# Attention, a three-way-maximum layer and a gated layer on one core: the whole first layer moved behind the attention, quarter-array products for the last keys, wider exponentials

## The chip, the cores and the metric

The kernel runs on one core of a Trainium2 chip. The metric is the device time of one execution in microseconds; lower is better. Engines are named as in the profile: PE is TensorE (matrix products; PEld its weight loads), DVE is VectorE, ACT is ScalarE, POOL is GpSimd, SP the queue from which nearly all DMAs are issued. Every matrix product of the program streams 384 or 448 columns. An fp32 matmul shows as two weight loads and two MATMUL records; a product in fp32r shows as one of each.

## The reference

```python
scores = q @ k.T / 8;  scores = 30 * tanh(scores / 30)     # 4 batches x 12 heads, 448 x 448
attn = exp(scores - max);  attn /= attn.sum(-1) + 1e-9
x = (attn @ v).transpose(0, 2, 1, 3).reshape(1792, 768)
h = maximum(maximum(x @ w1, x @ w2), x @ w3)               # first layer, 768 -> 768
y = h @ w_out                                              # second layer, 768 -> 768
out = (sigmoid(y @ w_gate) * (y @ w_val)) @ w_out2         # third 768 -> 1536, fourth 1536 -> 768
```

The weights arrive as eight-byte floats, and are decoded on ACT and DVE (five instructions a block) to fp32. Every product of the layers is split in high and low fp32r halves, and takes three passes (high x high, high x low, low x high).

## The kernel before, in words

**Attention.** A batch has 448 rows: three groups of 128 keys and a rest of 64. Heads go in pairs, 24 in all, and a pair's two heads lie in partitions 0 to 63 and 64 to 127. `scores` (L296 on) gives, per pair, one full-array product for the rest of the keys (L312) and three groups of two half-array products (L315; each head uses its 64 rows of the array and its own PSUM bank). ACT takes tanh of each of the four results (L320), then exp (L334). `weigh` (L346 on) multiplies the weights with v, two column halves of the array at a time (L353); `total` (L356 on) sums the weights over the keys with a matrix of ones (L364; the first six pairs also L362 for the rest, later pairs add the rest on DVE, L343). `finish` (L367 on) transposes the totals on DVE, takes the reciprocal and multiplies. For the last eight pairs q and k are split, and the scores take three fp32r passes.

**First layer before.** `Layer1` does batches 0 and 1 as plain products: for each of 6 column blocks j and 3 matrices, 18 matmuls per batch (648 in all). They are interleaved with the attention from pair 7 on, and the last of them run just behind it. `Layer1Pair` then does batches 2 and 3 as seven block products (Strassen-Winograd): nine triples of column-block pair and matrix, each of 7 products of 9 matmuls (567 in all, L556). A block product needs sums of the two batches' halves (`making`, `cut`, L973 to L985) and sums of the weights' quarters (L527 to L530), each split in high and low (L535, L536).

**Order.** `PROGRAM` writes out, by letters and per pair, in which order PE, DVE and ACT get their instructions (`manual_schedule`): F is `finish`, S storing x split, U adding up the sums, 1 the first sum, P, W and O a plain first-layer product, its weights and its evacuation, d one third of a decoding, X the next pair's preparation. 24 weight blocks are decoded during the attention, and 8 more after it. DMAs wait in the SP queue in the order of issue. Everything after the attention is ordered by the scheduler's priorities.

**Block products.** `Blocks.run` (L540 on) goes through the triples; `prepare` splits the weights of a product into a ring of three buffers, two products ahead; `after` evacuates: ACT copies three of the seven results (L575), DVE adds three (L580), and `out` takes the maximum on DVE. `hooks` hang other work behind a named product.

Of the kernel before, what the change touches and what calls it, by code (L numbers as in the profile page):

```python
# [17 lines left out]
def tile_kernel(ctx: ExitStack, tc: tile.TileContext, q, k, v, cap, w1, w2, w3, wo, wg, wv, wo2, out):  # L18
# [15 lines left out]
    MAKING = (1, 1, 1, 1, 1, 1, 1, 1, 1, 1, 1, 1)  # L34
    ROOMS = {1: 8, 2: 9, 6: 10, 5: 11, 7: 12, 3: 13, 4: 14}
    SOON = 24
    ONESX = (0, 1, 2, 3, 4, 5)
# [3 lines left out]
        0: ("", "d1UddXd"),  # L41
        1: ("", "1FXUS"),
        2: ("dd", "F1SUXd"),
        3: ("d1d", "FUSXd"),
        4: ("dd", "d1FSUX"),
        5: ("dd1", "FSdUX"),
        6: ("dd", "1FSUXdd"),
        7: ("F1", "BdPSWUdOX"),
        8: ("ddF", "PS1WUdXO"),
        9: ("ddFd1", "PXWSUOd"),  # L50
        10: ("ddF", "1PXWSUdO"),
        11: ("ddF", "1WSPXUddO"),
        12: ("dF", "d1PXWSUddO"),
        13: ("ddF1", "PWSOPXWUddddO"),
        14: ("ddF", "W1PSOPXWUddddO"),
        15: ("ddF", "P1WSOPXWUdO"),
        16: ("dF", "Sd1PWOXPWUdO"),
        17: ("ddF", "1PWSOPXWUO"),
        18: ("ddF", "1PWXSUOPWddO"),
        19: ("dd", "F1PWSOPXWUdO"),  # L60
        20: ("dF1", "PWSOPXWUdO"),
        21: ("d", "F1PWSOPXWOU"),
        22: ("F", "1PWSOPXWUO"),
        23: ("Fd", "1PWSOPWUOPXWO"),
        24: ("d", "FPWSOPWOPWO"),
    }
    PLAIN = (0, 1, 2, 3, 4, 5, 6, 7, 8, 9, 10, 11, 12, 13, 14, 15)
# [5 lines left out]
    us = dram.tile([B, NF, P, S], F32, name="us")  # L73
    ws2 = dram.tile([NF, P, DM], F32, name="ws2")
# [87 lines left out]
    class Rooms:  # L162
# [5 lines left out]
        def flat(self, n, name, dt=F32R):  # L168
            return self.pools[n // 8].tile([P, KC * S], dt, tag=f"room{n}", name=name, bufs=1)
# [27 lines left out]
    def load_pair(n, pools, begin=None):  # L197
        ld, wk, ep, pp, mm, (ident, ones, onesx, capb, tsc, kfs, vss, vts) = pools
# [12 lines left out]
        nc.sync.dma_start(out=kf[:, : NT * P], in_=kk[:, : NT * P])  # L211
# [3 lines left out]
        for e in range(2):  # L215
            own = slice(e * D, (e + 1) * D)
            nc.sync.dma_start(out=kf[own, NT * P + e * TAIL : NT * P + (e + 1) * TAIL], in_=kk[own, NT * P :])
        nc.sync.dma_start(out=vs, in_=main(v))
        for e in range(2):
            nc.sync.dma_start(out=vx[e * TAIL : (e + 1) * TAIL, e], in_=rest(v)[e])  # L220
        return qf, kf

    def prepare(n, loaded, pools):


        ld, wk, ep, pp, mm, (ident, ones, onesx, capb, tsc, kfs, vss, vts) = pools
        qf, kf = loaded
        if n in PLAIN:
            return kf, qf
        kh = wk.tile([P, SK], F32R, tag="kh", name="kh")  # L230
        nc.scalar.copy(kh, kf)
        kl = wk.tile([P, SK], F32R, tag="kl", name="kl")
        nc.vector.tensor_sub(kl, kf, f(kh))
        qh = wk.tile([P, S], F32R, tag="qh", name="qh")
        nc.scalar.copy(qh, qf)
        ql = wk.tile([P, S], F32R, tag="ql", name="ql")
        nc.vector.tensor_sub(ql, qf, f(qh))
        return kh, kl, qh, ql

# [4 lines left out]
    def less_max(es, pools):  # L244

        ld, wk, ep, pp, mm, (ident, ones, onesx, capb, tsc, kfs, vss, vts) = pools
        for e in es:
            nc.vector.tensor_scalar_mul(e, e, capb)
        for h in range(2):
# [4 lines left out]
            top = pp.tile([P, 512], F32, tag="pv", name="top", bufs=2)  # L254
            for c in range(NT + 1):
                cols = slice(c * P, min((c + 1) * P, S))
                n = cols.stop - cols.start
                turned = pp.tile([P, 2, 512], F32, tag="sc", name="turned")[:, 0]
# [23 lines left out]
    class Pair:  # L282


        def __init__(self, n, prepared, pools, xb, general):
            self.n, self.prepared, self.pools, self.xb, self.general = n, prepared, pools, xb, general
            self.e, self.sum = {}, None

            self.alone = n < NP and not general
            self.whole = n in ONESX and not general  # L290
            self.own = general

        def scores(self, groups, add=True):

            ld, wk, ep, pp, mm, (ident, ones, onesx, capb, tsc, kfs, vss, vts) = self.pools
            if self.n in PLAIN:  # L296
                terms = (self.prepared,)
            else:
                kh, kl, qh, ql = self.prepared
                terms = ((kh, qh), (kl, qh), (kh, ql))  # L300
            last = len(terms) - 1
            banks = []
            for c in groups:
                if c is None and not self.own:
                    pool, tag = (mm, "mm") if self.n <= NP else (pp, "pv")
                    sc = pool.tile([P, 512], F32, tag=tag, name="rest", bufs=2).unsqueeze(1)
                else:
                    sc = pp.tile([P, 2, 512], F32, tag="sc", name="sc")
                banks.append(sc)
                for m, (kk, qq) in enumerate(terms):  # L310
                    if c is None:
                        nc.tensor.matmul(sc[:, 0, :S], kk[:, NT * P : SK], qq, start=(m == 0), stop=(m == last))  # L312
                        continue
                    for j, own in enumerate(HALVES):
                        nc.tensor.matmul(sc[:, j, :S], kk[own, c * P : (c + 1) * P], qq[own], start=(m == 0), stop=(m == last))  # L315
            for c, sc in zip(groups, banks):
                w = 1 if c is None else 2
                e = ep.tile([P, w, S], F32, tag=f"e{w}", name="e", bufs=7 if w == 2 else 3)
                self.e[c] = e
                nc.scalar.activation(e, sc[:, :w, :S], AF.Tanh, scale=tsc)  # L320
            if not self.general:
                for c in groups:
                    self.weights(c, add)

        def add_first(self):
            ld, wk, ep, pp, mm, (ident, ones, onesx, capb, tsc, kfs, vss, vts) = self.pools
            self.sum = ep.tile([P, 2, S], F32, tag="sum", name="sum", bufs=2)
            nc.vector.tensor_add(self.sum, self.e[0], self.e[1])

        def weights(self, c, add=True):  # L330

            ld, wk, ep, pp, mm, (ident, ones, onesx, capb, tsc, kfs, vss, vts) = self.pools
            e = self.e[c]
            nc.scalar.activation(e, e, AF.Exp, scale=1.0 if self.general else capb)  # L334
            if c == 1 and add:
                self.add_first()

        def add_up(self):
            nc.vector.tensor_add(self.sum, self.sum, self.e[2])
            if self.whole:  # L340
                return
            for j, own in enumerate(HALVES):
                nc.vector.tensor_add(self.sum[own, j], self.sum[own, j], self.e[None][own, 0])  # L343
# [11 lines left out]
        def total(self):  # L355

            ld, wk, ep, pp, mm, (ident, ones, onesx, capb, tsc, kfs, vss, vts) = self.pools
            if self.alone:
                self.pv.append(mm.tile([P, 512], F32, tag="mm", name="pv"))
# [6 lines left out]
        def finish(self):  # L366
# [6 lines left out]
            if self.general:  # L373
                nc.vector.tensor_scalar_add(inv, r[:, :, 0], 1e-9)
# [450 lines left out]
    def compute(own: ExitStack, general, once):  # L825
# [138 lines left out]
        for _ in ahead:  # L964
            pass
# [247 lines left out]
```

## Time and profile before

| | us |
|---|---|
| median of 3 runs | 1003.03 (1000.75 to 1008.34) |
| profiled execution, its own time | 1000.76 |
| its span | 998.9 |
| PE busy | 984.5 |
| DVE busy | 783.0 |
| ACT busy | 532.6 |
| POOL busy | 43.3 |
| first scores start | 5.23 |
| Layer1Pair starts | 322.3 |
| second layer starts | 437.0 |
| third layer starts | 527.2 |

The profiled execution is the source of all durations; what lies outside its span is 1000.76 - 998.9 = 1.86 us. Stages are read from the first product of each line: L312, L556, L194 (`h`), L556 again. A weight load's start on PEld marks the place of its product, and the step from one start to the next is the time a product takes.

### The profile page before, as it was taken

The page shows a single profiled execution, that of the slowest core. Times are in us where ns is not written, and L with a number is a line of the kernel's source. Part 1 is how long each engine was busy: PE and PEld are TensorE (multiplying, and loading weights), DVE is VectorE, ACT ScalarE, POOL GpSimd, SP SyncE. Part 2 cuts the span into 40 slices and gives each one's busy share as a digit, 9 for nine tenths or more (in the row PEclk, how much of TensorE's full clock was granted, in tenths as well). Part 3 has the DMA queues.
Part 4 walks back from the last instruction along what each step waited for, and adds up shares of the span by engine and source line. Part 5 has one row for each costly group of instructions (what it writes and reads, how often), then busy time and mean ns, then how long its engine had stood idle before and what let it go on. Part 6 is the DMA issues. An engine that isn't in the chain of part 4 may idle for free.

```text
span 998.9 us, 13705 instructions
## 1 busy us (share of the span) xinstructions
PE 984.5 (99%) x4946; PEld 818.0 (82%) x4946; DVE 783.0 (78%) x1283; ACT 532.6 (53%) x817; POOL 43.3 (4%) x49
## 2 busy tenths in 40 slices
PE   8999999999999999999999999999999999999997
PEld 3335566667778999989989999988999989999997
DVE  3999999888779877776879878788888689785661
ACT  7987876777646454444337444434343344533330
POOL 1000000000000000015520000000000000000000
PEclk9999999999999999999999999999999999999999
DMA  6877577645324211136343446555456676421331
GB/s 197 262 231 255 183 245 270 218 130 176 95 80 131 89 56 57 45 112 207 138 133 91 136 143 184 161 166 175 157 156 198 213 241 241 167 79 48 100 107 59
DMA packets 87868, 153.17 MB, mean 153 GB/s; under 512 B 32624, under 2 KB 60144, under 8 KB 87792
## 3 DMA queue, kind: packets, MB, share of 16 engines
q1 hardware_dynamic: 87360, 151.88, 48.2%
q8 instruction: 41, 0.67, 0.3%
q10 hardware_dynamic: 432, 0.33, 0.1%
q14 instruction: 35, 0.29, 0.1%
HBM read 113.64 MB, written 38.54 MB: 152 GB/s over the span
## 4 chain that ended last, share of the span: by engine, by line
PE 79%; DVE 11%; DMA 5%; ACT 2%; issue 2%; SPq 1%; DVEq 0%; ACTq 0%
PE mm L556 37%; PE mm L728 15%; PE mm L194 14%; PE pv L353 6%; PE sc L315 4%; DMA ws<-wd 1%; PE pv L364 1%; DVE wd L137 1%; PE rest L312 1%; DVE wd L138 1%; DMA wf<-ws 1%; DVE wd L135 1%; DVE wd L134 1%; DVE wl L148 1%; DVE temps L580 1%
## 5 line engine op out<-in xcount | busy, mean ns | idle before, releaser
L556 PE MATMUL mm<-part,ring 128*128 128x448 f32 x2079 | 424.2, 366 | 2.8 <-DVE temps L580 1.4
L556 PEld LDWEIGHTS mm<-part,ring 128*128 128x128 f32 x2079 | 389.9, 188 | 36.7 <-DVE temps L580 2.6
L194 PE MATMUL mm<-x,wh 128*128 128x448 f32 x432 | 95.7, 370 | 1.0 <-ACT wh L147 0.9
L194 PEld LDWEIGHTS mm<-x,wh 128*128 128x128 f32 x432 | 79.5, 188 | 17.0 <-issue 8.1
L728 PE MATMUL mm<-w2a,u 128*128 128x384 f32 x504 | 88.1, 334 | 0.0
L728 PEld LDWEIGHTS mm<-w2a,u 128*128 128x128 f32 x504 | 87.4, 188 | 0.1
L334 ACT ACTIVATE e<-e,capb 128x448 f32<-128x448 f32 (+1 forms) x96 | 86.2, 946 | 0.7
L320 ACT ACTIVATE e<-sc,tsc 128x896 f32<-128x896 f32 x72 | 70.0, 1004 | 16.5 <-PE sc L315 16.2
L535 ACT CAST ring<-w 128x384 fp32r<-128x384 f32 x92 | 46.7, 510 | 48.4 <-PE mm L556 38.9
L580 DVE TENSOR_TENSOR temps<-mm,temps 128x448 f32<-128x448 f32 x91 | 56.1, 618 | 13.7 <-PE mm L556 12.8
L728 PE MATMUL mm<-w2b,u 128*128 128x384 f32 x378 | 66.0, 334 | 0.0
L728 PEld LDWEIGHTS mm<-w2b,u 128*128 128x128 f32 x378 | 65.6, 188 | 0.0
L194 PE MATMUL mm<-h,wh 128*128 128x448 f32 x288 | 63.3, 368 | 0.6 <-ACT wh L147 0.6
L712 ACT CAST u<-u 128x1344 fp32r<-128x1344 f32 x24 | 31.7, 1323 | 56.8 <-PE mm L728 51.1
L575 ACT COPY temps<-mm 128x448 f32<-128x448 f32 x91 | 48.0, 532 | 24.8 <-PE mm L556 12.0
L353 PE MATMUL pv<-e,vs 128*64 128x448 f32 x288 | 59.4, 548 | 0.0
L194 PEld LDWEIGHTS mm<-h,wh 128*128 128x128 f32 x288 | 53.9, 188 | 6.4 <-ACT wh L147 1.3
L535 ACT CAST ring<-s 128x384 fp32r<-128x384 f32 x69 | 35.2, 511 | 43.8 <-PE mm L556 42.3
L536 DVE TENSOR_TENSOR ring<-s,ring 128x384 fp32r<-128x384 f32 x69 | 38.1, 553 | 21.7 <-PE mm L556 12.7
L536 DVE TENSOR_TENSOR ring<-w,ring 128x384 fp32r<-128x384 f32 x92 | 51.0, 555 | 4.2 <-ACT ring L535 3.1
L713 DVE TENSOR_TENSOR u<-u,u 128x1344 fp32r<-128x1344 f32 x24 | 37.1, 1552 | 17.6 <-ACT u L712 17.6
L194 PE MATMUL mm<-x,wl 128*128 128x448 f32 x216 | 49.6, 365 | 0.0
(159 smaller groups left out, 1284.5 us busy)
## 6 DMA issues: line engine op xcount, KB each, us to landing
wraw<-in_moe_w_dram SPq DMA_DIRECT2D x18, 768.0 KB, 5.2
wf<-ws SPq DMA_DIRECT2D x36, 384.0 KB, 3.4
w<-ws SPq DMA_DIRECT2D x30, 384.0 KB, 3.0
us<-temps SPq DMA_DIRECT2D x48, 224.0 KB, 2.6
u<-us SPq DMA_DIRECT2D x8, 1344.0 KB, 7.7
ws<-wd SPq DMA_DIRECT2D x26, 384.0 KB, 2.7
qf<-in_q_dram SPq DMA_DIRECT2D x23, 224.0 KB, 5.1
kf<-in_k_dram SPq DMA_DIRECT2D x24, 192.0 KB, 4.6
```

The costliest lines, as they stand in the source:

```text
L194: nc.tensor.matmul(ps, a[:, c, :], at(x, m, c), start=(n == 0), stop=(n == len(passes) - 1))
L315: nc.tensor.matmul(sc[:, j, :S], kk[own, c * P : (c + 1) * P], qq[own], start=(m == 0), stop=(m == last))
L320: nc.scalar.activation(e, sc[:, :w, :S], AF.Tanh, scale=tsc)
L334: nc.scalar.activation(e, e, AF.Exp, scale=1.0 if self.general else capb)
L353: nc.tensor.matmul(self.pv[0][own, :S], lhs, e, start=(c == 0), stop=(c is None))
L535: nc.scalar.copy(w[:, 0], src)
L536: nc.vector.tensor_sub(w[:, 1], src, f(w[:, 0]))
L556: nc.tensor.matmul(ps, w[:, wm, c, :], x[:, xm, c, :], start=(q == 0 and not onto), stop=(q == len(order) - 1), skip_group_check=bool(onto),)
L575: nc.scalar.copy(c[i], ps)
L580: add(c[n], ps, c[n])
L713: nc.vector.tensor_sub(self.part[h][1][:, :, cols], src[:, own], f(high))
L728: nc.tensor.matmul(ps, a, ww[g][:, w], start=(c == 0 and m == 0), stop=(c == KC - 1 and m == 2))
```

## The change

Layer 1 leaves the attention altogether. `Layer1` is now a `Blocks` class with the seven block products for both pairs of batches: three triples for batches 0 and 1 alone, six for both pairs, three for batches 2 and 3 alone; 1134 matmuls. Its results go to DRAM (`hd`), and the second layer fetches them from there (`fetch`) and splits them (`split_h`). The sums of the x blocks (`Parts`, eleven steps a pair of batches) run on DVE in the attention from pair 13 on (letters m, M), and the last two of the first pair and nine of the second in the hooks of the first three triples (`MAKING`).

In the attention the rest of the scores (`rest`) is two 64x64 products, one per head, in opposite quarters of the array; the totals of the rest (`rest_total`) take the two other quarters, and land in the other head's partitions, so `total` and `finish` swap halves. The rest times v (`weigh`) is two quarter products. All 24 pairs use fp32 scores. ACT takes tanh over rest and group 0 in one instruction (1344 columns), tanh over group 1, exp over all of these (2240), and tanh and exp over group 2, one pair later. PSUM holds one tile of three banks (`three`), one of two (`two`), one for the totals (`low`) and two others (`mm`). 12 weight blocks are decoded in the attention instead of 24, 12 in halves in the middle of layer 1, and 8 as before in the second layer.

The letters of the new table: C second (group 2) of the pair before, A begin (group 0), R the rests and rest totals, Q weigh, U the second sum, B first (group 1), V weigh_group, T total, F finish, 1 the first sum, L the start of layer 1.

```diff
-        4: ("dd", "d1FSUX"),
+        4: "CARUBQVTddFd1",
...
-        14: ("ddF", "W1PSOPXWUddddO"),
+        14: "CARQUBVTmdF1dd",
...
-        24: ("d", "FPWSOPWOPWO"),
+        24: "CLRQUVTF",
...
+    NEAR = 2
+    MAKING = ((0, 5), (0, 7), (0, 7), (1, 1), (1, 6), (1, 5), (2, 1), (2, 7), (2, 7))
...
+        def rest(self, own):
+            qf, kf = self.loaded
+            nc.tensor.matmul(self.three[own, 0, :S], kf[own, NT * P :], qf[own], start=True, stop=True)
+        def rest_total(self, own, other):
+            nc.tensor.matmul(self.pv[1][other, :S], ones[own, :D], self.e[None][own, 0], start=True, stop=True)
+        def first(self):
+            two = pp.tile([P, 2, 512], F32, tag="two", name="sc")
+            self.scores(1, two)
+            e = ep.tile([P, 5, S], F32, tag="e5", name="e")
+            self.e = {None: e[:, :1], 0: e[:, 1:3], 1: e[:, 3:]}
+            nc.scalar.activation(e[:, :3], self.three[:, :, :S], AF.Tanh, scale=tsc)
+            nc.scalar.activation(e[:, 3:], two[:, :, :S], AF.Tanh, scale=tsc)
+            if not self.general:
+                nc.scalar.activation(e, e, AF.Exp, scale=capb)
...
+            for own in HALVES:
+                nc.tensor.matmul(self.pv[0][own, :S], vts[self.n % 4][own], self.e[None][own, 0], start=True, stop=True)
...
+            self.steps = [
+                lambda: cut(1, xa[:, tops]),
+                lambda: sub(xa[:, tops], xc[:, tops], xa[:, tops]),
+                lambda: sub(xc[:, tops], xc[:, ends], xc[:, tops]),
+                lambda: cut(3, xc[:, ends]),
...
-            super().__init__([(j, w, (0,)) for j in range(HC) for w in range(3)], (parts,), mm, wpool, hooks)
+            quads = [(0, w, (0,)) for w in range(3)]
+            quads += [(j, w, (0, 1)) for j in range(1, HC) for w in range(3)]
+            quads += [(0, w, (1,)) for w in range(3)]
...
+            if w == 2:
+                nc.sync.dma_start(out=hd[2 * p + i % 2, 2 * j + i // 2], in_=held)
...
+        at_ += [((0, i), parts[0].step) for i, _ in zip(l1.ORDER, parts[0].steps)]
+        at_ += [((k, i), parts[1].step) for k, i in MAKING]
...
+        def other(j):
+            if j < 4:
+                b, e = places[j]
+                fetch(hb[b][e], b + 2, e)
+            if j > 1:
+                b, e = places[j - 2]
+                split_h(hb[b][e])
```

**PE, one of the early pairs, before.** `rest`, `sc` are the scores of the pair, `pv` the weighted values and totals of the pair before.

```order
L312 MATMUL rest<-qf,kf_111 128x448
L315 MATMUL sc<-qf,kf_111 128x448 x4
L353 MATMUL pv<-e,vs_128 64x448 x6
L353 MATMUL pv<-e,vx_129 64x448 x2
L315 MATMUL sc<-qf,kf_111 128x448 x2
L362 MATMUL pv<-e,onesx 64x448 x2
L364 MATMUL pv<-sum,ones 64x448 x2
```

Ten steps of the array, if a step is one full product, two halves or up to four quarters; from pair 7 on one or two groups of 18 first-layer products (L194) follow here.

**PE, one pair, now** (the first row is the pair before's last scores; L282 are the quarter products of the rest, L287 the quarter totals).

```order
L272 MATMUL sc_310<-qf_156,kf2_118 128x448 x2
L272 MATMUL sc_322<-qf_194,kf0_112 128x448 x2
L282 MATMUL sc_322<-qf_194,kf0_112 64x448
L287 MATMUL pv_326<-e_276,ones_123 64x448
L282 MATMUL sc_322<-qf_194,kf0_112 64x448
L287 MATMUL pv_326<-e_276,ones_123 64x448
L351 MATMUL pv_325<-e_276,vx2_120 64x448 x2
L272 MATMUL sc_334<-qf_194,kf0_112 128x448 x2
L358 MATMUL pv_325<-e_276,vs2_119 64x448 x4
L358 MATMUL pv_325<-e_313,vs2_119 64x448 x2
L364 MATMUL pv_326<-sum_305,ones_123 64x448 x2
```

Nine steps, and nothing but the attention stands on PE until the last pair.

**DVE, first block products of layer 1, before** (`ring` is a weight split, `s` and `w1` the weight sums, `part` a split of x sums, `temps` an evacuation).

```order
L536 TENSOR_TENSOR ring_2996<-s_3006,ring_2996 128x384
L580 TENSOR_TENSOR temps_3019<-mm_3038,temps_3019 128x448
L536 TENSOR_TENSOR ring_2996<-w1_3000,ring_2996 128x384
L536 TENSOR_TENSOR ring_2997<-s_3006,ring_2997 128x384
L974 TENSOR_TENSOR part_2885<-x_1277,part_2885 128x1344
L536 TENSOR_TENSOR ring_2996<-w1_3000,ring_2996 128x384
L527 TENSOR_TENSOR s_3118<-w1_3013 128x384
```

**The same place now**, from the last pair's product with its reciprocal (L381) on.

```order
L381 TENSOR_TENSOR x_1197<-pv_1541,xn_1561 128x448
L400 TENSOR_TENSOR x_1197<-x_1197 128x1344
L548 TENSOR_TENSOR temps_1576<-mm_1596,temps_1576 128x448
L395 TENSOR_TENSOR part_1591<-x_507,part_1591 128x1344
L504 TENSOR_TENSOR ring_1524<-w1_1278,ring_1524 128x384
L504 TENSOR_TENSOR ring_1525<-s_1530,ring_1525 128x384
L395 TENSOR_TENSOR part_1698<-x_863,part_1698 128x1344
L395 TENSOR_TENSOR part_1607<-x_162,part_1607 128x1344
L504 TENSOR_TENSOR ring_1524<-w1_1278,ring_1524 128x384
L548 TENSOR_TENSOR temps_1576<-mm_1580,temps_1576 128x448
L504 TENSOR_TENSOR ring_1524<-w1_1535,ring_1524 128x384
```

Before, one wide instruction (1344 columns) stood between the ring's splits here, the others were done under the plain products; now four stand in this piece, and eleven before the fourth triple's first split, with 42 small ones.

## Rows read from the trace of the kernel before

**Rows 1.** The page: busy time of each engine; granted clock in 40 slices.
```profile
PE 984.5 (99%) x4946; PEld 818.0 (82%) x4946; DVE 783.0 (78%) x1283; ACT 532.6 (53%) x817; POOL 43.3 (4%) x49
PEclk9999999999999999999999999999999999999999
```
**Rows 2.** Windows by stage: length, busy time of each engine (instructions), clock, DMA.
```profile
13.40:72.40 59.00, 58.33 (x265) 19.82 (x263) 52.07 (x83) 54.46 (x66) 0.00 (x0) 1.00 0.81 253
...
322.30:437.00 114.70, 114.70 (x567) 106.29 (x567) 87.86 (x164) 54.71 (x105) 2.04 (x1) 1.00 0.21 61
437.00:482.00 45.00, 44.58 (x217) 40.31 (x217) 31.35 (x37) 20.25 (x35) 23.12 (x14) 1.00 0.55 185
...
527.20:838.70 311.50, 308.68 (x1512) 283.21 (x1511) 258.55 (x535) 142.57 (x288) 0.00 (x0) 1.00 0.55 170
```
**Rows 3.** Timeline of PEld, one early pair: start, duration, instructions, idle time before.
```profile
52.87 0.30 PEld L312 LDWEIGHTS rest<-qf,kf 128*128 128x128 f32 x2 [0.70 <-DMA vx<-in_v_dram]
...
55.53 0.20 PEld L353 LDWEIGHTS pv<-e,vs 128*64 128x64 f32 x4 [0.65 <-issue]
55.96 0.14 PEld L353 LDWEIGHTS pv<-e,vs 128*64 128x64 f32 x2 [0.23 <-issue]
...
57.84 0.14 PEld L353 LDWEIGHTS pv<-e,vx 128*64 128x64 f32 x2 [0.23 <-issue]
58.69 0.30 PEld L315 LDWEIGHTS sc<-qf,kf 64*128 64x128 f32 x4 [0.70 <-ACT e L334]
59.64 0.20 PEld L362 LDWEIGHTS pv<-e,onesx 128*64 128x64 f32 x4 [0.65 <-DVE wd L138]
...
61.29 0.30 PEld L312 LDWEIGHTS rest<-qf,kf 128*128 128x128 f32 x2 [0.70 <-DMA vs<-in_v_dram]
```
**Rows 4.** Timeline of ACT, an early pair.
```profile
46.07 0.61 ACT L320 ACTIVATE e<-rest,tsc 128x448 f32<-128x448 f32 x1
46.59 1.89 ACT L320 ACTIVATE e<-sc,tsc 128x896 f32<-128x896 f32 x2
48.37 2.53 ACT L334 ACTIVATE e<-e,capb 128x448 f32<-128x448 f32 x3
...
53.34 0.89 ACT L132 ACTIVATE wd<-wraw 128x768 f32<-128x768 f32 x1
```
**Rows 5.** Lines of DVE, 13.4 to 72.4 us: count, busy us, mean ns, idle before.
```profile
L328 DVE TENSOR_TENSOR sum<-e 128x896 f32<-128x896 f32 x7 | 7.6, 1085 | 0.3 <-ACT e L334 0.3
...
L137 DVE SCALAR_TENSOR_TENSOR wd<-wraw,wd 128x768 int32<-128x768 int32 x6 | 5.7, 954 | 0.0
...
L371 DVE STREAM_TRANSPOSE r<-pv 128x448 f32<-128x448 f32 x7 | 4.5, 646 | 0.8 <-PE pv L364 0.8
...
L379 DVE TENSOR_TENSOR xn<-pv,xn 128x448 f32<-128x448 f32 x7 | 4.3, 618 | 0.1
L135 DVE TENSOR_SCALAR wd<-wd 128x768 int32<-128x768 int32 x7 | 3.8, 549 | 0.1
...
L375 DVE RECIPROCAL inv<-r 128x14 f32<-128x14 f32 x7 | 1.7, 242 | 0.2
```
**Rows 6.** Lines of the whole run: DVE's evacuation, weight split and wide split.
```profile
L580 DVE TENSOR_TENSOR temps<-mm,temps 128x448 f32<-128x448 f32 x91 | 56.1, 618 | 13.7 <-PE mm L556 12.8
...
L536 DVE TENSOR_TENSOR ring<-w,ring 128x384 fp32r<-128x384 f32 x92 | 51.0, 555 | 4.2 <-ACT ring L535 3.1 <-PE mm L556 1.0
...
L974 DVE TENSOR_TENSOR part<-x,part 128x1344 fp32r<-128x1344 f32 x5 | 7.7, 1552 | 0.0
```
**Rows 7.** Timeline of the start: the first scores and their tanh.
```profile
5.23 0.99 PE L312 MATMUL rest<-qf,kf 128*128 128x448 f32 x2
...
6.26 0.64 ACT L320 ACTIVATE e<-rest,tsc 128x448 f32<-128x448 f32 x1 [3.08 <-PE rest L312]
```
**Rows 8.** Waits of ACT, 13.4 to 160 us: total, times, longest.
```profile
ACT wd L132 <- DMA wraw<-in_moe_w_dram: 3.2, 5, 1.2
```
**Rows 9.** Timeline of DVE in the second layer, POOL busy beside it.
```profile
445.48 2.49 DVE L137 SCALAR_TENSOR_TENSOR wd<-wraw,wd 128x768 int32<-128x768 int32 x1
```

More of the change, by code (lines that the diff above doesn't have):

```diff
@@ L293, in scores @@
[L293 to L320, printed above, removed]
-            if not self.general:
-                for c in groups:
-                    self.weights(c, add)
@@ new lines, in second, with all @@
+        def second(self):
+            ld, wk, ep, pp, mm, (ident, ones, capb, tsc, kfs, vss, vts) = self.pools
+            two = pp.tile([P, 2, 512], F32, tag="two", name="sc")
+            self.scores(2, two)
+            e = self.e[2] = ep.tile([P, 2, S], F32, tag="e2", name="e")
+            nc.scalar.activation(e, two[:, :, :S], AF.Tanh, scale=tsc)
+            if not self.general:
+                nc.scalar.activation(e, e, AF.Exp, scale=capb)
+        def all(self):
+            self.begin()
+            for own in HALVES:
+                self.rest(own)
+            self.first()
+            self.second()
+            self.less()
+            self.add_first()
+            self.add_up()
+            self.open()
+            for own, other in (HALVES, HALVES[::-1]):
+                self.rest_total(own, other)
+            self.weigh()
+            for c in range(NT):
+                self.weigh_group(c)
+            self.total()
+            self.finish()
@@ L926, in run @@
                         {
-                            "P": l1.product,
-                            "B": lambda: l1.split(0),
-                            "W": l1.following,
-                            "O": l1.out,
-                            "S": before and before.store,
+                            "C": before and (lambda: [before.second(), load(n + 2)]),
+                            "A": more and pair.begin,
+                            "R": rests,
+                            "B": more and pair.first,
@@ L1024, in build @@
[L1024 to L1035 removed]
+        for x in parts:
+            x.early = False
+        mm = l1.mm = Banks((six, mm, *[six] * 5, mm))
@@ L1078, in compute, with build, temps @@
+        def build(i, src, n):
+            later[i] = rooms.half(n, "part")
+            for c in range(HC):
+                split(later[i], c, src[c] if isinstance(src, list) else src[:, c])
+        def temps(n):
+            t = rooms.chunks(n, "temps")
+            return [t[:, c] for c in range(KC)]
+        tops, ends = slice(0, HC), slice(HC, KC)
+        l4 = Layer4(pairs, rooms, mm, wpool, sm)
+        end = len(l3.quads) - 1
         formed = []
```

528 lines of the change are left out of this document (248 added, 280 removed).

## The prediction

> **What bounds the kernel now.** I read the page first: PE is busy for 984.5 of 998.9 us, DVE for 783.0, ACT for 532.6, and the granted clock is full from end to end [rows 1]. So time can only be won where PE gets less to do, and is lost wherever PE is made to wait. The windows by stage say where the other engines come near: in the attention before the first layer starts (13.4 to 72.4 us) DVE is busy for 52.07 of 59.00 us and ACT for 54.46, with DMA at 0.81; in the block products of the first layer DVE is busy for 87.86 of 114.70 [rows 2]. These are the two places where the change takes cover away. Last I read the timelines of one pair for what a step of PE, ACT and DVE costs there [rows 3, 4, 5].
>
> **PE's work.** 648 plain and 567 block matmuls become 1134 block matmuls, 81 fewer. A block matmul costs 114.70 / 567 = 0.2023 us in a stage without idle time [rows 2], so the new first layer is 1134 x 0.2023 = 229.4 us of PE, and 81 x 0.2023 = 16.4 us of work is gone.
>
> **A pair on PE.** In [rows 3] five half steps take 57.84 - 55.96 = 1.88 us, so a step (two column halves side by side) takes 0.75 us. The period from one pair's rest to the next is 61.29 - 52.87 = 8.42 us: ten steps, 7.5 us, and five changes of the array's division at 0.18; the single step from 58.69 to 59.64 gives 0.95 - 0.75 = 0.20 for a change. Now there are nine steps (6.75) and four changes (0.8): 7.55 us. That counts four quarter products as one step. No row shows a quarter product. Its bounds: four at once are one step, as two column halves are now, and one head after the other is two steps. I take one step, since [rows 3] are nearest: there two halves run at once with different moving data and into the same PSUM bank.
>
> The Trainium skill, TensorEngine Tiling (Array Packing), section Restrictions and Gotchas, speaks against this: "Different row tiles cannot access same PSUM bank simultaneously." The two rests are different row tiles and write into one bank, and so do the two quarter products with v. By that rule the rests and the products with v would cost two steps each, and the sum would be that of rival 3, 1027 us; no row of before shows it or speaks against it, since its row halves, the scores, write into two banks.
>
> **A pair on ACT.** From [rows 4]: a tanh over 448 is followed by the next after 0.52 us, two over 896 take 48.37 - 46.59 = 1.78; so 448 columns cost 0.37 and an instruction 0.15. Three exps over 2240 columns in all take 2.53, or about 0.40 for 448. No row has the wide forms; from these, tanh over 1344 is 1.26, two tanhs over 896 are 1.78, exp over 2240 is 2.15 and over 896 is 0.95: 6.1 us, with 0.89 for a decoding's first step 7.0. If every duration counts in full, 7.4. Either is under PE's 7.55.
>
> **A pair on DVE.** From [rows 5]: two sums at 1.085, two transposes at 0.646, two reciprocals at 0.242, a product at 0.618, and for a decoding two TENSOR_SCALAR at 0.55 and two SCALAR_TENSOR_TENSOR at 0.954: 4.6 + 3.0 = 7.6 us in the twelve pairs that decode, 4.6 plus at most two wide ones of up to 1.55 [rows 6] in the others. So for twelve pairs DVE is as long as PE.
>
> **The new wait.** PE does the first quarter rest and then waits for the exp over 2240 columns of the pair before (`rest_total`). Behind it on PE stand the weighing, the next scores and the totals; ACT's next wide tanh waits for the rests, and DVE's `finish` for the totals. Nothing else fills PE. ACT's round from exp to exp is 6.1 to 7.4 us, within PE's 7.55, so PE arrives last and the wait is short. I take 7.55 a pair for 22 pairs and 8.6 for the first, whose program puts the weighing before the next scores, behind an exp.
>
> **Sum to the end of the first layer.** The first scores start at 5.23, and tanh comes 6.26 - 5.23 = 1.03 after a step's start, that is 0.28 after its 0.75 [rows 7]. Now two steps and a change precede the first tanh: 5.23 + 0.75 + 0.2 + 0.75 + 0.28 = 7.2; tanh 1.26, tanh 0.89, exp 2.15 and its end bring the first exp to 11.7. The last pair's exp ends at 11.7 + 8.6 + 22 x 7.55 = 186.4. Then come the last pair's rest total, its weighing (four steps more) and three changes, 5 x 0.75 + 3 x 0.2 = 4.3 us, and the first block product at 190.7; the last total, which in the new order stands behind that product, costs a step and a change, 0.95. With 229.4 the layer would end at 421.0.
>
> **DVE at the start of layer 1.** The fourth triple's first weight split has 11 wide and 42 small DVE instructions and a `finish` ahead of it, after the last second sum, which I put 7.2 us behind the last exp. At 1.5, 0.5 to 0.55 and 2.4 us [rows 5, 6] that is 40 to 42 us, so DVE is there 47 to 49 us behind that exp. PE would be there after 4.3 + 0.95 us and three triples, 189 x 0.2023 = 38.2: 43.5. PE loses 3.5 to 5.5 us, and some more where a split stands behind a wide one in the order; bounds 2 and 10, I take 5. From the fourth triple on a product has twice the matmuls per weight split, and DVE has room: half of a decoding is some 1.6 us, four a triple, against 126 x 0.2023 = 25.5 us of PE.
>
> The third layer, of the same kind, left PE idle for 311.50 - 308.68 = 2.8 us in 1512 matmuls [rows 2]; for 945 such ones I add 1.7. The layer ends at 421.0 + 5 + 1.7 = 427.7 instead of 437.0: 9.3 us won.
>
> **Behind it.** The second layer gets four fetches, four wide ACT casts and four wide DVE subtractions, 6.2 us [rows 6], beside 45.00 - 31.35 = 13.7 us in which DVE is idle there [rows 2]. With POOL busy a DVE instruction of 0.954 took 2.49 [rows 5, 9], which would make 16 us of the 6.2, more than the cover. Bounds 0 and 4, I take 1. The 48 stores to DRAM and the later decodings lie in a stage with DMA at 0.21, and become like the third layer's, 0.55 [rows 2]: nothing. Two small transfers of k less per pair, in a stage where PE hardly waits for a DMA, are worth nothing either. All else is unchanged.
>
> Sum: 1000.76 - 9.3 + 1 = 992.5 us, against the profiled execution's own time, which lies at the lower end of the three runs (median 1003.03). I forecast 992 us, **1.1% below the median**; 1% is about what a measurement here can tell from no change, so this is on the line between faster and same.
>
> **Rivals.**
> 1. *All of PE's saving arrives.* DVE's backlog is hidden by the ring and the eight banks, and instructions overlap so that a pair takes 7.4. For: 16.4 us of work and five changes' share less. That gives 992.5 - 5 - 1.7 - 23 x 0.15 = 982. Against: the ring is only two products ahead. Chance 0.15.
> 2. *The three engines of a pair are coupled.* At 7.55, 7.4 and 7.6 none has slack, and DMA at 0.81 is pressed closer; ACT waited five times for raw weights, up to 1.2 us [rows 8], and an Abs that waits now holds up tanh and with it PE. If the twelve decoding pairs take 8.2 and the others 7.8, 12 x 0.65 + 11 x 0.25 = 10.6 us are lost: 1003. It decides from 7.95 a pair on, where the gain is gone. Chance 0.17.
> 3. *Quarters of one bank run one after the other: slower.* The rests and the products with v then take a step more each, 2 x 0.75 x 23 = 34.5 us, which nothing fills, as PE is the longest of the three: 1027. If only one of the two does, 17 us: 1010. It turns the sign as soon as 9 us, a quarter of it, come true. For: no row has row halves in one bank. Against: two column halves do share one, in other partitions, as here. Chance 0.13. The sentence of the Trainium skill quoted above (TensorEngine Tiling (Array Packing)) states this case.
>
> The forecast itself (985 to 999) has 0.55. Range: 982 to 1010, which leaves out the better half of rival 1 and most of rival 3, under 2 in 10. Faster by over 1% (below 993): rival 1 and half of the forecast's share, 0.15 + 0.28 = 0.43. Slower by over 1% (above 1013): most of rival 3 and the end of rival 2, 0.15. Same: 0.42.
>
> **What would show it.** PEld's rests come 7.5 to 7.6 us apart in pairs 2 to 23, with one LDWEIGHTS group of four quarters per step; ACT's exp over 2240 columns takes about 2.2 us. The first seven-product matmul starts near 191 us, and PE's waits in the next 45 us name DVE's or ACT's weight split, some 5 us in all. The second layer starts near 428. It is wrong if the rests take 1.5 us, if a pair takes 8 us with PE idle behind exp, DVE's sum or a DMA, or if PE's waits in the first three triples pass 10 us.

## The result, and the profile after

| | before | changed kernel |
|---|---|---|
| median of 8 runs each, us | 1003.73 (1000.75 to 1008.34) | **993.6** (989.47 to 996.19) |
| ratio | | 0.9897, interval 0.9871 to 0.9922 |
| profiled execution, its own time | 1000.76 | 991.71 |
| its span | 998.9 | 989.8 |
| PE busy | 984.5 | 968.5 |
| first block product of layer 1 | | 189.15 |
| second layer's first product on PE (its weight load stands at 437.0 before) | 437.23 | 426.06 |
| third layer's first product | 527.17 | 516.80 |

The change makes the kernel 1.0% faster, 0.8 to 1.3% by the interval. 992 us was forecast.

The page of the changed kernel, the rows that answer to [rows 1]: busy time of each engine, and the granted clock.

```profile
PE 968.5 (98%) x4929; PEld 794.1 (80%) x4929; DVE 775.8 (78%) x1310; ACT 502.6 (51%) x723; POOL 40.4 (4%) x31
PEclk9999999999999999999999999999999999999999
```

PE has 16.0 us less to do (16.4 were worked out), and is idle for 989.8 - 968.5 = 21.3 us where it was idle for 14.4. The gain in the span, 9.1 us, is 16.0 - 6.9. So the question is where 6.9 us of PE's time went. By stage, PE is idle for 8.1 us up to the second layer (4.2 before), 2.4 in the second layer (0.6), 2.9 in the third (2.8) and 8.0 from the fourth on (6.8).

Windows by stage of the changed kernel, the columns of [rows 2]: two stretches of the attention, the start of layer 1, its steady part, the second layer.

```profile
44.53:96.00 51.47, 51.47 (x278) 17.91 (x278) 47.51 (x71) 49.47 (x41) 0.00 (x0) 1.00 0.76 237
96.00:186.00 90.00, 90.00 (x486) 30.57 (x486) 81.04 (x112) 78.81 (x63) 0.00 (x0) 1.00 0.35 99
189.00:228.20 39.20, 34.99 (x169) 30.49 (x168) 37.99 (x59) 22.07 (x35) 0.00 (x0) 1.00 0.17 51
228.20:383.00 154.80, 154.80 (x765) 143.31 (x764) 119.08 (x241) 57.45 (x113) 0.00 (x0) 1.00 0.43 130
426.00:516.70 90.70, 88.31 (x434) 80.88 (x433) 69.65 (x82) 41.72 (x70) 37.45 (x23) 1.00 0.57 197
```

In the attention PE has no idle time left, though ACT (49.47 of 51.47) and DVE (47.51) are close behind it. In the first 39 us of layer 1 it is the other way round: DVE is busy for 37.99 of 39.20 us and PE for 34.99.

Timeline of PEld in one pair (compare [rows 3]), the four quarters of the rests and totals and what follows:

```profile
52.00 0.13 PEld L282 LDWEIGHTS sc<-qf,kf 64*64 64x64 f32 x1 [0.65 <-issue]
52.01 0.13 PEld L287 LDWEIGHTS pv<-e,ones 64*64 64x64 f32 x1
52.01 0.13 PEld L282 LDWEIGHTS sc<-qf,kf 64*64 64x64 f32 x1
52.02 0.13 PEld L287 LDWEIGHTS pv<-e,ones 64*64 64x64 f32 x1
...
52.43 0.15 PEld L351 LDWEIGHTS pv<-e,vx 64*64 64x64 f32 x2 [0.22 <-issue]
...
53.66 0.30 PEld L272 LDWEIGHTS sc<-qf,kf 64*128 64x128 f32 x4 [0.71 <-ACT e L309]
...
59.47 0.13 PEld L282 LDWEIGHTS sc<-qf,kf 64*64 64x64 f32 x1 [0.65 <-issue]
```

All four quarter products start within 0.02 us, the two rests among them, which lie in different row halves and write to one PSUM bank. The pair takes 59.47 - 52.00 = 7.47 us; 17 of the 23 steps from one pair's rests to the next take just that.

Timeline of ACT in the same pair (compare [rows 4]):

```profile
45.89 1.36 ACT L296 ACTIVATE e<-sc,tsc 128x1344 f32<-128x1344 f32 x1
47.26 1.01 ACT L297 ACTIVATE e<-sc,tsc 128x896 f32<-128x896 f32 x1
48.30 2.17 ACT L299 ACTIVATE e<-e,capb 128x2240 f32<-128x2240 f32 x1
50.37 0.91 ACT L132 ACTIVATE wd<-wraw 128x768 f32<-128x768 f32 x1
51.37 1.01 ACT L307 ACTIVATE e<-sc,tsc 128x896 f32<-128x896 f32 x1
52.41 1.04 ACT L309 ACTIVATE e<-e,capb 128x896 f32<-128x896 f32 x1
```

From L296 to the next L296 at 53.35 it is 7.46 us, with short pauses alone: the wide exp takes 2.17 us (2.15 was estimated), the wide tanh 1.36 (1.26), and ACT is the engine with the least room beside PE.

PE at the end of the attention, and DVE beside it:

```profile
189.15 2.12 PE L524 MATMUL mm<-part,ring 128*128 128x448 f32 x9
193.02 0.97 PE L364 MATMUL pv<-sum,ones 128*64 128x448 f32 x4 [1.75 <-DVE sum L341]
194.84 5.51 PE L524 MATMUL mm<-part,ring 128*128 128x448 f32 x24 [0.84 <-DVE r L371]
...
211.61 4.72 PE L524 MATMUL mm<-part,ring 128*128 128x448 f32 x22 [1.47 <-ACT ring L503]
```
```profile
187.43 1.08 DVE L338 TENSOR_TENSOR sum<-e 128x896 f32<-128x896 f32 x1
188.46 1.03 DVE L504 TENSOR_TENSOR ring<-w,ring 128x384 fp32r<-128x384 f32 x2
...
191.41 0.55 DVE L504 TENSOR_TENSOR ring<-s,ring 128x384 fp32r<-128x384 f32 x1
191.87 1.09 DVE L341 TENSOR_TENSOR sum<-sum,e 128x896 f32<-128x896 f32 x1
```

The last pair's second sum (L341) waits on DVE behind seven small instructions for the ring and the weight sums, and the last totals on PE (L364) wait for it; the next block product then waits for the transpose that frees their bank. Later PE waits once more, 1.47 us, for a ring split. L503 is ACT's half of a split; on ACT it stands behind a wide cast (L394) that had waited for a wide subtraction on DVE:

```profile
209.84 1.31 ACT L394 CAST part<-x 128x1344 fp32r<-128x1344 f32 x1 [0.76 <-DVE x L402]
```

### The profile page after: what moved, and what is told of

It reads as the page before. It is cut to its first block, busy times and chain, and to the rows that moved or that the text cites. A ratio compares the mean times of both kernels' runs of the same rounds, so it can differ in the third digit from the quotient of the medians.

```text
span 989.8 us, 13549 instructions
## 1 busy us (share of the span) xinstructions
PE 968.5 (98%) x4929; PEld 794.1 (80%) x4929; DVE 775.8 (78%) x1310; ACT 502.6 (51%) x723; POOL 40.4 (4%) x31
## 4 chain that ended last, share of the span: by engine, by line
PE 74%; DVE 11%; DMA 9%; ACT 3%; issue 2%; ACTq 0%; SPq 0%; DVEq 0%
PE mm L524 41%; PE mm L698 15%; PE sc L272 6%; PE pv L358 5%; PE sc L282 2%; DMA ws<-wd 2%; PE pv L364 2%; PE pv L351 2%; PE mm L194 1%; DMA raw<-in_moe_w_val_dram 1%; DVE wd L137 1%; DMA w2a<-ws 1%; ACT wd L132 1%; DVE ring L504 1%; DVE temps L548 1%
## 5 line engine op out<-in xcount | busy, mean ns | idle before, releaser
L524 PE MATMUL mm<-part,ring 128*128 128x448 f32 x2646 | 540.3, 366 | 5.7 <-ACT temps L543 1.9
L524 PEld LDWEIGHTS mm<-part,ring 128*128 128x128 f32 x2646 | 495.7, 188 | 50.9 <-ACT temps L543 5.0
L548 DVE TENSOR_TENSOR temps<-mm,temps 128x448 f32<-128x448 f32 x115 | 71.1, 620 | 18.8 <-PE mm L524 18.4
L503 ACT CAST ring<-w 128x384 fp32r<-128x384 f32 x104 | 52.6, 509 | 64.6 <-PE mm L524 51.7
L543 ACT COPY temps<-mm 128x448 f32<-128x448 f32 x115 | 60.7, 531 | 39.8 <-PE mm L524 28.4
L272 PE MATMUL sc<-qf,kf 64*128 64x448 f32 x288 | 67.6, 573 | 2.1 <-ACT e L297 1.6
L194 PE MATMUL mm<-h,wh 128*128 128x448 f32 x288 | 62.6, 366 | 2.4 <-ACT wh L147 2.4
L503 ACT CAST ring<-s 128x384 fp32r<-128x384 f32 x78 | 39.5, 510 | 45.9 <-PE mm L524 39.1
L504 DVE TENSOR_TENSOR ring<-w,ring 128x384 fp32r<-128x384 f32 x104 | 57.7, 556 | 4.9 <-PE mm L524 3.6
L194 PEld LDWEIGHTS mm<-h,wh 128*128 128x128 f32 x288 | 53.9, 188 | 7.7 <-ACT wh L147 3.5
L272 PEld LDWEIGHTS sc<-qf,kf 64*128 64x128 f32 x288 | 23.8, 187 | 45.0 <-issue 24.6
L299 ACT ACTIVATE e<-e,capb 128x2240 f32<-128x2240 f32 x24 | 52.0, 2166 | 0.8
L358 PEld LDWEIGHTS pv<-e,vs 128*64 128x64 f32 x288 | 18.5, 136 | 38.1 <-issue 32.1
L148 POOL TENSOR_TENSOR wl<-wf,wh 128x768 fp32r<-128x768 f32 x12 | 25.4, 2121 | 457.6 <-DVE ring L504 407.6
```

The source lines that it names most:

```text
L194: nc.tensor.matmul(ps, a[:, c, :], at(x, m, c), start=(n == 0), stop=(n == len(passes) - 1))
L272: nc.tensor.matmul(ps[:, j, :S], kf[own, c * P : (c + 1) * P], qf[own], start=True, stop=True)
L299: nc.scalar.activation(e, e, AF.Exp, scale=capb)
L358: nc.tensor.matmul(self.pv[0][own, :S], vs[:, c, j], self.e[c][:, j], start=False, stop=True, skip_group_check=True)
L503: nc.scalar.copy(w[:, 0], src)
L504: nc.vector.tensor_sub(w[:, 1], src, f(w[:, 0]))
```

## Experiments

The runs' medians have intervals some 0.5% wide, so most of what follows is read from positions in the traces: the time from the start of the attention's last scores to a given block product of layer 1, found by counting the starts of L524. In products alone (4.3 us to the first, 0.95 for the last totals, 0.2023 each) the 190th, the first of the fourth triple, would stand at 43.5.

| us from the last scores to | 10th | 37th | 127th | 190th | second layer |
|---|---|---|---|---|---|
| changed kernel | 9.96 | 15.91 | 35.96 | 48.73 | 241.19 |
| act_low | 9.96 | 15.92 | 35.53 | 48.29 | 240.93 |
| u_first | 8.94 | 14.67 | 35.68 | 48.45 | 242.45 |
| no_low | 9.96 | 18.32 | 36.55 | 49.33 | 241.67 |
| u_first_no_low | 8.94 | 15.89 | 34.56 | 47.58 | 243.45 |
| pool_low | 9.96 | 15.94 | 48.65 | 61.41 | 253.95 |

**same_quarter: the rest totals share the rests' quarters.**

```diff
-            nc.tensor.matmul(self.pv[1][other, :S], ones[own, :D], ...)
+            nc.tensor.matmul(self.pv[1][own, :S], ones[own, :D], ...)
...
```

> The rest totals are put into the same quarter of the array as the rest of their own head (total and finish swap back), so quarter products no longer run four at a time: two steps of 0.75 us where the changed kernel has one. Theory (PE bounds the pair, four quarters are one step): the pair goes from 7.47 to 8.2 us, 23 x 0.75 = 17 us slower than the changed kernel's 993.6, about 1010. Rival (the pair is bound by the chain through exp, and PE has slack): under 5 us slower, below 999. Rival (quarters never ran together): no change.

Measured: 1010.34 us (1008.98 to 1013.63), ratio to before 1.0066 (1.0041 to 1.009). PE, one pair:

```profile
71.07 0.98 PE L282 MATMUL sc<-qf,kf 64*64 64x448 f32 x4
71.87 0.93 PE L287 MATMUL pv<-e,ones 64*64 64x448 f32 x4
72.62 0.93 PE L351 MATMUL pv<-e,vx 64*64 64x448 f32 x4
...
79.29 0.98 PE L282 MATMUL sc<-qf,kf 64*64 64x448 f32 x4
```

The totals now start 0.80 us behind the rests, and a pair takes 8.22 us, 0.75 more. It is shown that the use of the two idle quarters is worth 0.75 us a pair, some 17 us, and that without it the change would have been a loss: this is the place at which rival 3 would have turned the sign.

**no_rest_v: one step of PE less.** The product of the rest with v is left out of the weighing; the first group's product begins the sum in its place.

```diff
-            for own in HALVES:
-                nc.tensor.matmul(self.pv[0][own, :S], vts[self.n % 4][own], self.e[None][own, 0], ...)
+            return
...
```

> Leaves out the rest's product with v (two quarter products, one step of 0.75 us a pair). Theory (PE bounds a pair, but DVE and ACT stand just under it, at 7.4 in the twelve decoding pairs and 6.2 to 7.1 in the others): about 12 x 0.1 + 11 x 0.5 = 7 us faster, 985 to 989. Rival (PE alone matters): 23 x 0.75 = 17 us faster, 976. Rival (PE does not bound the pair): no change.

Measured: 984.13 us (979.62 to 989.36), ratio 0.9786 (0.9753 to 0.9819). That is just past the expected 985 to 989, and far from the 976 of PE alone. In the trace the 23 steps from rest to rest add up to 164.99 us instead of 172.34, 7.4 less where 7 were expected. In the late pairs, which do not decode, the steps are 6.73 us, again 0.75 less than 7.47. In pairs that decode they vary between 6.7 and 8.1, where the wide exps often follow each other at 7.14, ACT's own round, and PE is idle for 2.09 of 47.50 us:

```profile
44.50:92.00 47.50, 45.41 (x230) 14.45 (x228) 44.11 (x67) 44.46 (x38) 0.00 (x0) 1.00 0.87 279
```

So PE bounds the changed kernel's pairs, but in the decoding ones by a few tenths only: with 0.75 us less on it, PE waits between 11 and 176 us for DVE's second sum (2.2 us in all) and for ACT (1.1), where the changed kernel has 0.6 for ACT alone. That is near rival 2's case, though only 0.3 us of ACT's waits there are for raw weights.

**narrow_exp: the wide tanh and exp in pieces of 448 and 896.**

```diff
...
-                nc.scalar.activation(e, e, AF.Exp, scale=capb)
+                for own in (slice(0, 1), slice(1, 3), slice(3, 5)):
+                    nc.scalar.activation(e[:, own], e[:, own], AF.Exp, scale=capb)
```

> The tanh over 1344 columns and the exp over 2240 are cut into the old pieces (448, 896, 896), three ACT instructions more a pair. Theory: ACT goes from 6.2 to 6.7 us a pair (7.1 to 7.6 where a decoding stands on it), at or under PE's 7.47, so 0 to 3 us slower, 993 to 997. Rival (the wide forms carry the gain): 3 x 0.15 x 24 = 11 us slower, about 1004.

Measured: 993.69 us (991.13 to 995.0), ratio 0.9894 (0.9866 to 0.9923); a later pair still takes 7.47. ACT's busy time grows by 11.1 us. In the attention PE waits 4.1 us for ACT where it waited 2.0, all of it in the early pairs, and the 23 steps add up to 173.0 us instead of 172.3: the wide exponentials, a third of the change by its name, are worth nothing measurable here.

**act_low: the late low halves are taken from DVE.**

```diff
-                sub(to[:, 1], src, f(to[:, 0]))
+                if self.early:
+                    sub(to[:, 1], src, f(to[:, 0]))
+                else:
+                    nc.scalar.copy(to[:, 1], src)
```

> In the first three triples of layer 1 the low halves of the x sums are not subtracted on DVE but copied by ACT (so the low halves are wrong): eight wide DVE instructions, 12 us, less there. Theory (DVE's backlog makes PE idle for 4.2 of the first 39 us): PE idle there falls to 2.6 or less, what is left being the last total's wait; 1.5 to 3 us faster, about 991. Rival (the order of the ring or ACT's queue): no change or slower, since ACT gets 10 us more.

Measured: 994.58 us (990.42 to 996.76), ratio 0.9912 (0.9887 to 0.9937). DVE is busy for 7.4 us less from 189 to 228.2, and the 190th product comes only 0.4 us earlier; PE's idle time there is 3.8 us, where 2.6 or less was expected and the changed kernel has 4.2:

```profile
189.00:228.20 39.20, 35.43 (x171) 31.02 (x170) 30.64 (x54) 32.26 (x45) 0.00 (x0) 1.00 0.22 66
```

The expectation failed. But ACT, which got the copies, rose by 10.2 us, and a wait of 1.00 for its evacuation (temps L546) took the place of the wait for the ring. The run moved the load instead of removing it, and decides nothing; no_low below is the better form.

**u_first: the last second sum ahead of the ring's splits.**

```diff
-        24: "CLRQUVTF",
+        24: "CURQLVTF",
```

> Program 24 has the last pair's second sum ahead of the start of layer 1 ("CURQLVTF"): on DVE the sum over the last keys comes straight behind the first one, before the ring's splits, and on PE the last totals come before the first block product. Theory: about 3 of the 6.4 us that the new first layer loses stem from that sum, which starts at 191.87 behind 4.4 us of the ring's work while the totals wait for it, and not from DVE being full. Then the wait for the sum (1.7 us) and most of the 0.84 us behind it go: 1.5 to 3 us faster than the changed kernel, 991 to 992 us where it has 993.6, the second layer at 423 to 424.5 instead of 425.9. Rival: DVE is busy for 38 of 39.2 us there, so the ring's splits come that much later, and PE waits for them instead: 993 to 995, the same sum of waits.

Measured: 993.8 us (992.28 to 998.5), ratio 0.99 (0.9871 to 0.9929). PE:

```profile
190.65 0.97 PE L364 MATMUL pv<-sum,ones 128*64 128x448 f32 x4 [0.54 <-DVE sum L341]
...
209.97 0.87 PE L524 MATMUL mm<-part,ring 128*128 128x448 f32 x3 [0.43 <-DVE ring L504]
211.26 1.49 PE L524 MATMUL mm<-part,ring 128*128 128x448 f32 x6 [0.41 <-ACT ring L503]
212.92 2.74 PE L524 MATMUL mm<-part,ring 128*128 128x448 f32 x12 [0.18 <-ACT ring L503]
215.87 0.47 PE L524 MATMUL mm<-part,ring 128*128 128x448 f32 x1 [0.21 <-ACT temps L543]
```

The wait for the sum fell from 1.75 to 0.54 us, and PE is 1.0 us ahead at the 10th product and 1.2 at the 37th. At the 127th it is 0.3: from the 37th to the 127th u_first takes 21.01 us and the changed kernel 20.05, and the four waits for splits and an evacuation have taken the gain back. The theory, that this sum's place costs 3 us of its own, fell; the rival holds. That suggests that what DVE has to do in all, more than the order in which it does it, sets the point that PE reaches; no_low tests it.

**u_first_p1: as u_first, and the second pair's next scores ahead of its weighing.**

```diff
-        1: "CARQUVBTdFdd1",
+        1: "CARQUBVTdFdd1",
```

> As u_first, and in the second pair's program the next scores stand before the weighing, as in the others ("CARQUBVTdFdd1"). Theory: the 8.47 us from the second rests to the third, against 7.47 elsewhere, are ACT waiting for these scores behind the weighing; with them first the step takes 7.5 to 7.9: 0.6 to 1.0 us faster than u_first, some 990.5 us, below what the timing can tell, so it is read from the starts of the rests. Rival: the third pair's Abs, which waited 0.97 us for its raw weights in the next step, waits that much longer instead, and nothing is won by the fourth pair.

Measured: 993.96 us (991.17 to 995.97), ratio 0.9892 (0.9865 to 0.992). Against u_first, the step in question went from 8.47 to 8.05, where 7.5 to 7.9 was expected, the next from 8.02 to 7.65, and the third from 8.44 to 8.67; the four early steps together from 32.95 to 32.39, 0.6 us less. The third pair's Abs, ACT's first step of a decoding, now waits 1.98 us (1.18 in u_first) and starts 0.10 us after its raw weights have landed: the wait that the rival named, which takes back a part of the gain and not all of it. The two medians, 993.96 and 993.8, can't tell this.

**no_low: DVE's late wide subtractions left out.**

```diff
-                sub(to[:, 1], src, f(to[:, 0]))
+                if self.early:
+                    sub(to[:, 1], src, f(to[:, 0]))
+                else:
+                    part[i] = to[:, :1].to_broadcast([P, 2, HC, S])
```

> The changed kernel without the low halves of the seven late x parts (DVE's wide subtractions behind the attention; the products read the high half in their place, so they do the same work on other numbers). Nothing is put on ACT for it, unlike in act_low, where ACT took the copies over and PE waited for ACT's evacuations instead. From the start of the last scores of the attention to the 190th block product (the fourth triple's first) the changed kernel takes 48.7 us, where the products alone need 43.5. Theory, DVE's backlog of 40 us of work sets that point: with 7 x 1.5 = 10 us less of it, what is left of the 5.3 us lost is the wait around the last sum, 2.5 to 3 us: 46 to 46.5, and the whole 2 to 3 us faster, 991. Rival, the loss is ACT's and the ring's depth: 48 or more, and no change in the whole.

Measured: 992.39 us (991.29 to 994.49), ratio 0.9876 (0.9848 to 0.9904), within the noise of the changed kernel's 993.6. DVE has eight instructions fewer, not seven (1302 where the changed kernel has 1310), and is busy for 9.7 us less in all. The 190th product stands at 49.33, by itself a miss. PE and then the windows show why (columns as above, PEclk before the DMA share):

```profile
193.69 0.97 PE L364 MATMUL pv<-sum,ones 128*64 128x448 f32 x4 [1.78 <-DVE sum L341]
195.51 39.73 PE L527 MATMUL mm<-part,ring 128*128 128x448 f32 x181 [0.84 <-DVE r L371]
```
```profile
195.50:201.50 6.00, 5.99 (x16) 5.35 (x17) 4.29 (x7) 3.05 (x4) 0.00 (x0) 0.50 0.00 1
201.50:233.00 31.50, 31.50 (x156) 29.17 (x156) 27.59 (x53) 22.72 (x38) 0.00 (x0) 1.00 0.44 133
```

Behind the two waits at the last sum PE has no wait at all in the first three triples: the 2.4 us that it lost there, mostly to a ring split, are gone. From the 37th to the 127th product it takes 18.23 us, which is what the products alone need (90 x 0.2023 = 18.2), where the changed kernel takes 20.05. But in this execution the granted clock was 0.50 (1.2 GHz) from 195.5 to 201.5, and 16 products took 6.00 us instead of 16 x 0.2023 = 3.24. Without these 2.8 us the 190th product would stand at 46.6, by estimate, at the edge of the theory's 46 to 46.5.

**u_first_no_low: both.** The edits are those of u_first and no_low.

> As no_low, with the second sum ahead of the ring's splits as in u_first. In u_first the 1.2 us won by the 37th block product were 0.3 by the 127th, where PE waited for DVE's and ACT's ring splits. Theory, DVE's backlog took them back: with 10 us less on DVE the win at the front stays, and the way from the last scores to the 190th product is 44 to 45.5 us, against 48.5 in u_first: 3 to 4 us faster than the changed kernel, 990. Rival, the ring's depth and ACT set that point whatever DVE has to do: 47.5 to 48.5, no change.

Measured: 993.12 us (992.47 to 994.45), ratio 0.9874 (0.985 to 0.9899). The 190th stands at 47.58: by the number that is the rival's 47.5 to 48.5. PE's waits from 183 to 235 us:

```profile
PE mm L527 <- issue: 1.2, 1, 1.2
PE mm L527 <- DVE r L371: 1.0, 1, 1.0
PE pv L364 <- DVE sum L341: 0.5, 1, 0.5
```

No wait for the ring is left here either. 1.2 us went to a pause before the 37th product, at 200.51, for which the profile names no engine. ACT shows it:

```profile
196.24 3.74 ACT L394 CAST part<-x 128x1344 fp32r<-128x1344 f32 x3
199.88 0.53 ACT L546 COPY temps<-mm 128x448 f32<-128x448 f32 x1
```

The 37th product adds to a bank whose sum so far ACT has to copy out first (L546). That copy stands behind three wide casts on ACT and ends 0.1 us before the product starts. So ACT's order costs this time, which is a part of what the rival said. The products also ran at 0.207 us instead of 0.203 all through layer 1 (see the last section), 0.7 us by the 190th. Less these two it would be 45.7, by estimate, just above what the theory gave.

**pool_low: the second pair of batches' low halves on POOL.**

```diff
-                sub(to[:, 1], src, f(to[:, 0]))
+                (sub if self.early or self.first else nc.gpsimd.tensor_sub)(to[:, 1], src, f(to[:, 0]))
...
```

> The low halves of the second pair of batches' x parts that are made behind the attention (wide subtractions, 1.5 us each) go to POOL instead of DVE; POOL does nothing else there. no_low showed that without these subtractions the ring's splits are in time. Theory: the 2.5 us in which PE waits for the ring in the first three triples go, the way from the last scores to the 190th block product is 46 to 47 us instead of 48.7, and the whole some 2 us shorter, which the timing can hardly tell. Rival: DVE's instructions take longer beside POOL, as one of 0.954 us took 2.49 in the second layer of the kernel before; then the ring's splits are as late as they were or later: 48.5 to 52, and no gain or a loss.

Measured: 1006.89 us (1004.43 to 1009.34), ratio 1.0024 (1.0003 to 1.0045): all of the change's gain is lost. The rival holds, and by more than it said: the 190th product stands at 61.41, where it had 48.5 to 52. POOL and DVE at one place:

```profile
199.65 3.16 POOL L395 TENSOR_TENSOR part<-x,part 128x1344 fp32r<-128x1344 f32 x1 [198.23 <-ACT part L394]
199.80 3.43 DVE L504 TENSOR_TENSOR ring<-w,ring 128x384 fp32r<-128x384 f32 x1
203.15 0.54 DVE L504 TENSOR_TENSOR ring<-s,ring 128x384 fp32r<-128x384 f32 x1
```

A ring split that takes 0.54 us alone takes 3.43 when POOL has begun a subtraction just before, and ends 0.4 us after POOL's. The Trainium skill, SBUF — State Buffer, section "SBUF: two separate sides", says that a VectorE instruction with two inputs in SBUF and a GpSimd instruction that reads SBUF exclude each other, the later one standing still until the first has ended; the 3.43 us agree. DVE's busy time hardly changed (38.15 of 39.20 us), with 36 instructions done instead of 59. It is a likely reason for the 2.49 us of [rows 9] too, which were not tried by themselves.

## Why the prediction was right, point by point

| term of the sum | worked out | measured |
|---|---|---|
| PE's saving | 16.4 | 15.1 busy up to the second layer, 16.0 in all |
| first exp ends | 11.7 | 12.2 |
| last exp ends | 186.4 | 185.04 |
| a pair, steady | 7.55 | 7.47 |
| first block product | 190.7 | 189.15 |
| fourth triple's first split on DVE, behind the last exp | 47 to 49 | 230.88 - 185.04 = 45.8 |
| lost up to the 190th product | 5 (2 to 10) | 48.73 - 43.45 = 5.3 |
| lost from there on | 1.7 | 241.19 - 48.73 - 945 x 0.2023 = 1.3 |
| second layer starts | 427.7 | 426.06 |
| from there to the end, against before | +1 | 563.8 - 561.7 = +2.1 |
| profiled execution | 992.5 | 991.71 |

**Quarters.** That four quarter products are one step decided the sign, and held: the pair takes 7.47 us, one step more makes it 8.22 (same_quarter) and one less 6.73 (no_rest_v), each 0.75 apart. Nine steps at 0.75 leave 0.72 for four changes of the array's division, 0.18 each, where 0.20 was taken: that is the 0.08 a pair. The sentence of the Trainium skill that was weighed against it (TensorEngine Tiling (Array Packing), Restrictions and Gotchas) says that different row tiles can't use one PSUM bank at the same time; here two row tiles wrote to one bank, in different partitions, with starts 0.02 us apart and at no cost. The measurement decides, and rival 3 is out.

**Coupling.** Rival 2 did not come about, but by little: ACT's own round with a decoding is 7.14 us (no_rest_v; 7.0 to 7.4 was worked out), PE's 7.47. DVE's 7.6 was worked out too high, and above the 7.55 that the sum took: it is busy for 47.51 of 51.47 us, or 6.9 of 7.47. From exp to exp the first five steps took 8.47, 7.16, 8.22, 7.13 and 7.26, in all 38.2 us, where 8.6 + 4 x 7.55 = 38.8 was forecast; the 8.22 has a wait of 1.0 us for raw weights in it, the kind that rival 2 named. The other 18 took 7.48 on average.

**DVE's backlog.** The cause was right, the place only in part, and that the size came out at 5.3 where 5 was taken is partly luck. 9.96 - 4.27 - 0.95 - 9 x 0.2023 = 2.9 us appear at once, as waits around the last sum, for which the forecast had no term of its own. The other 2.4 come behind it, mostly at one ring split at 212 us, and none at the fourth triple, where the forecast put the loss: DVE begins that triple's first split at 230.88, 2.7 us before its product starts. From the start of the last sum to there it is busy for 37.6 us, where 40 to 42 were worked out behind that sum, and by the forecast's own reckoning PE would have lost 45.8 - 43.5 = 2.3 us.

That work on DVE sets this point is shown from both sides: a better order in front is taken back behind (u_first), with the subtractions left out PE's waits for the ring vanish (no_low, u_first_no_low), and with DVE held up by POOL the 190th product is 12.7 us later (pool_low; 2.4 us of it by estimate from 14 products at half clock). ACT's order has a part in it too (act_low, u_first_no_low).

**Mis-sized: behind the first layer.** 1 us was taken, 2.1 came. The second layer is 0.8 us longer (90.74 and 89.94), the third 0.3 shorter, and from the fourth on it is 1.6 longer. In the second layer PE's waits for ACT's weight casts have grown, here before and now:

```profile
PE mm L194 <- ACT wh L147: 0.6, 2, 0.4
PE mm L194 <- ACT wh L147: 2.4, 3, 1.2
```

So the new fetches, casts and subtractions may not be quite hidden there, and 1 us fits; no run parts them. The other wait is 7.5 us into the fourth layer, in code that the change does not touch:

```profile
834.86 0.83 ACT L672 CAST w2a<-w2a 128x768 fp32r<-128x768 f32 x1 [3.62 <-DMA w2a<-ws]
835.75 0.45 PE L698 MATMUL mm<-w2a,u 128*128 128x384 f32 x1 [1.57 <-ACT w2a L672]
```

ACT in turn waits for a DMA. The transfers around this boundary are issued as far ahead as before but land later: the last fetch of u, issued 3.45 us before the fourth layer's first product, takes 9.0 us where it took 6.6. The kernel before has no such wait, and every run of the changed kernel has one of 1.0 to 1.7 us but no_rest_v, whose code behind the attention is the same and where that fetch takes 6.6 us again. So it is not the new code as such; why the transfers take longer stays open.

**Which rival was nearest.** Rival 1, 982 us, wanted the backlog to be hidden; it was not. That the wide exponentials win nothing is no step of the forecast, which costed ACT as covered either way.

## What to carry to other kernels

When work leaves one stage for another, ask what each engine still owes at the boundary: here 16 us less on PE gave 9, most of the difference because DVE began the next stage with some 37 us of work and PE caught up with it. Reordering this backlog (u_first) only moved the wait; it has to become smaller, and POOL is no place to put it while DVE reads two operands from SBUF. Count a step of a divided array by its busiest quarter: here independent products in idle quarters cost nothing.

## What the runs showed of the hardware that was not expected

**Two paces at full clock.** The same block product takes 0.203 us in some stretches and 0.207 in others, with the granted clock at 1.00 and no wait. The same 60 us of the third layer, in the changed kernel and then in u_first, which have the same code there:

```profile
600.00:660.00 60.00, 60.00 (x298) 55.61 (x297) 52.86 (x118) 28.51 (x59) 0.00 (x0) 1.00 0.57 173
```
```profile
600.00:660.00 60.00, 60.00 (x292) 54.51 (x291) 52.03 (x115) 27.99 (x56) 0.00 (x0) 1.00 0.59 179
```

298 products against 292. A stretch keeps its pace for tens to hundreds of us. At the slower pace PE waited less (0.6 us in the third layer against 2.9), so that layer came to 313.2 us in u_first against 311.5. It may be one reason why executions of one kernel differ by some us, and it is why a gain of 1 or 2 us was read from positions. What picks the pace stays open.

**The clock after a short pause.** Around the last sum PE stood still for 1.78 and 0.84 us in no_low and got half clock for 6 us; in the changed kernel it stood still for 1.75 and 0.84 at the same place, and the clock stayed at 1.00, as it did in act_low after 1.78 and 0.84. same_quarter and no_rest_v have some nine products at 0.37 us behind the same place, after 1.04 and 2.05 us and again 0.84. So the small wait at the boundary can cost 1.5 to 2.8 us more than itself; what decides it can't be told from these runs.
